# Attention with a token-mixing MLP on one core: a dispatcher orders the engines, and part of the softmax exponentials is computed on VectorE

## The chip, the cores and the metric

The kernel runs on one core of a Trainium2 chip. The core has engines that work side by side, each through its own queue in order: TensorE (PE, matmuls, with weight loads shown as PEld), VectorE (DVE), ScalarE (ACT), GpSimd (POOL) and SyncE (SP, which here only issues DMAs). SBUF is the working memory of 128 partitions; PSUM is the memory that matmuls write, eight banks of 512 f32 columns. The metric is the time of one launch in microseconds (us), the median of several runs. A profile is one execution, whose span runs from the first to the last instruction.

## The reference

With x of 2048 rows by 512 columns, the output is `x + attention(xn) + mixer(xn)`:

```python
xn = _layernorm(x, axis=-1)
# attention: 32 heads of 16
qkv = (xn @ wqkv) ...                       # q, k, v per head
scores = einsum("bhqd,bhkd->bhqk", q, k) * 16 ** -0.5
o = einsum("bhqk,bhkd->bhqd", softmax(scores), v)
A = o.reshape(B, S, D) @ wo
# mixer: over the 2048 rows, with F = 1376
h = _layernorm(xn)
u = gelu(einsum("bsd,sf->bdf", h, w1) + b1) # tanh form
Bx = (einsum("bdf,fs->bds", u, w2) + b2).transpose(0, 2, 1)
```

## The kernel before

The scores are computed transposed: keys on the partitions, queries on the columns. A **block** is one of 4 query ranges of 512 times one of 8 sets of four heads, 32 blocks in all; in a block there are 16 key tiles of 128. One key tile of one block is a **group**, 512 in all. A group has four score matmuls of 32 rows each (`score_group`, L748), one head in each quarter of the array, into two pairs of PSUM banks; two exponentials over 128x1024 on ScalarE (`exp_pair`, L757) into the SBUF ring `pT` of ten buffers; and four matmuls `pv_group` (L767), each writing 32 partitions of PSUM bank 6, over all 16 key tiles. `V17` holds 16 values and a one for each head, so that the 17th row of each result is the softmax's denominator. Six banks form three pairs for scores, bank 6 gathers PV, bank 7 (`EX_BANK`) serves everything else.

At a block's end VectorE copies bank 6 to `OT32` (L688), shuffles the denominator row of each quarter over its 32 partitions (L695) and inverts it in four pieces of 128x128 (L700); GpSimd multiplies (L703) into `oT`. After eight blocks the out-projection (L652) of that query range can run. The mixer runs through bank 7 as well: 11 tasks `ut` (16 matmuls, L605, then a GELU on VectorE and ScalarE), 16 tasks `yt` (11 matmuls, L632, then two VectorE operations into an f32 `resid`), and 16 out-projections. Projections of Q, K and V (L425, L407, L569) are further tasks of that bank. The weights of the mixer are loaded by SP into two slots each (`task_w1_load`, `task_w2_load`); the eight loads of `wo_pad` are in `late_consts`.

The order of each engine's work is written out in Python while the kernel is built. Before, a loop counts periods, one group each: it emits the scores and exponentials of the group, the PV of the group two earlier, and at most two units of other matmuls (`EXTRA_BUDGET`) from a list with start periods (`sched_list`). `Sched` then gives each instruction the semaphore waits that its operands need. It keeps the last writer and the readers of a key, such as `("bank", 7)` or `("wo_pad", 3)`:

```python
        for k in writes:
            w = self.last_writer.get(k)
            if w is not None:
                deps.add(w)
            for r in self.readers.get(k, ()):
                deps.add(r)
```

A DMA is such an instruction too, and what waits for a DMA waits for its landing.

Of the kernel before, what the change touches and what calls it, by code (L numbers as in the profile page):

```python
# [12 lines left out]
S = 2048  # L13
# [13 lines left out]
GELU_A = 0.044715  # L27

DEBUG_SCHED = False
LAG = 2  # L30
NPB = 10
NQS = 3
EXTRA_BUDGET = 2.0
NW1 = 2
NW2 = 2

# [148 lines left out]
def bass_parallel_sum__softmax_full_mha__mixer_token_mlp__prompt_kernel(  # L185
# [18 lines left out]
    with ExitStack() as es:  # L204
# [5 lines left out]
        x_sb = sb("x_sb", [128, NT, D], BF16)  # L210
# [3 lines left out]
        resid = big.bitcast(F32)[:, :].rearrange("p (t d) -> p t d", d=D)  # L214

        def resid_alias_keys(st):
            ks = []
            for j in (2 * st, 2 * st + 1):
                ks.append(("xn", j) if j < NT else ("h", j - NT))
            return ks  # L220
# [6 lines left out]
        V17 = sb("V17", [128, NKT * H * 17 + 16], BF16)  # L227
        pT = sb("pT", [128, NPB, 1024], BF16)
        OT32 = sb("OT32", [128, 2, 512], F32)
        denb = sb("denb", [128, 2, 512], F32)  # L230
# [12 lines left out]
        u_sb = sb("u_sb", [128, 1, 512], F32)  # L243
        ga_sb = sb("ga_sb", [128, 1, 512], F32)
        osb = sb("osb", [128, 2, 512], BF16)
        ps = es.enter_context(nc.psum_tensor("ps", [128, 8 * 512], F32))

# [8 lines left out]
        def bank_bf16(i):  # L256
            return ps.bitcast(BF16)[:, i * 1024:(i + 1) * 1024] if hasattr(ps, "bitcast") else None

# [3 lines left out]
        def dma(q, dst, src, reads, writes, name="", noncontig=False):  # L262
            if noncontig:
                def fn(eng, dst=dst, src=src):
                    with nc.allow_non_contiguous_dma(reason="tiny strided vector load"):
                        return eng.dma_start(dst, src)
            else:
                def fn(eng, dst=dst, src=src):
                    return eng.dma_start(dst, src)
            return sc.add(q, fn, reads=reads, writes=writes, name=name, dma=True)  # L270
# [8 lines left out]
        v17_kh = V17[:, 0:NKT * H * 17].rearrange("p (k h c) -> p k h c", k=NKT, c=17)  # L279
        for T in range(1, 4):  # L280
            sc.add("dve", lambda e, T=T: e.memset(v17_kh[:, :, 8 * T, 0:16], 0.0),
                   writes=[("V", t, T) for t in range(NT)])
        sc.add("dve", lambda e: e.memset(V17[:, NKT * H * 17:], 0.0), writes=[("Vpad",)])
        sc.add("dve", lambda e: e.memset(v17_main[:, :, 16:17], 1.0), writes=[("Vone",)])

        sc.add("pool", lambda e: e.memset(qmask[:, 0:1], 0.0), writes=[("qmask",)])
        for r in range(4):
            sc.add("pool", lambda e, r=r: e.memset(qmask[32 * r:32 * r + 16, 0:1], 1.0),
                   reads=[("qmask",)], writes=[("qmask",)])
        sc.add("pool", lambda e: e.tensor_scalar(qmask[:, 1:2], qmask[:, 0:1], -1.0, 1.0, ALU.mult, ALU.add),  # L290
# [69 lines left out]
        def ln_tile(t, which):  # L360
            ln_stats(t, which)
            ln_norm(t, which)
# [12 lines left out]

        ps_bf = ps.bitcast(BF16)

        def kt_chunk(T, c, bk, evac_eng="dve"):
            kt_pe(T, c, bk)
            kt_evac(T, c, bk, evac_eng)  # L380

        def kt_evac(T, c, bk, evac_eng):
            evac(evac_eng, KT[:, T, 512 * c:512 * (c + 1)], bank(bk), reads=[("bank", bk)],
                 writes=[("KTt", T, t) for t in range(4 * c, 4 * c + 4)])
# [14 lines left out]
        def kt_pe(T, c, bk):  # L399
            for _ in kt_pe_gen(T, c, bk):  # L400
                pass

        def kt_pe_gen(T, c, bk):
            for ct in range(NCT):
                if ct % 2 == 0:
                    yield 2.0
                sc.add("pe", lambda e, ct=ct: e.matmul(  # L407
                    bank(bk), lhsT=wqkv_sb[:, ct, D + 128 * T: D + 128 * T + 128],
                    rhs=xnT[:, ct, 512 * c:512 * (c + 1)], start=(ct == 0), stop=(ct == NCT - 1)),
                    reads=[("wqkv", 1, T)] + [("xnT", t) for t in range(4 * c, 4 * c + 4)], writes=[("bank", bk)])  # L410

        def evac(eng, dst, src, reads, writes):
            if eng == "act":
                return sc.add("act", lambda e: e.activation(dst, src, ACTF.Identity), reads=reads, writes=writes)
            return sc.add("dve", lambda e: e.tensor_copy(dst, src), reads=reads, writes=writes)  # L415

        def qt_proj(qb, T, bk, act_first=False):
            for _ in qt_proj_gen(qb, T, bk, act_first):
                pass

        def qt_proj_gen(qb, T, bk, act_first=False):
            for ct in range(NCT):
                if ct % 2 == 0:
                    yield 2.0
                sc.add("pe", lambda e, ct=ct: e.matmul(  # L425
                    bank(bk), lhsT=wqkv_sb[:, ct, 128 * T:128 * (T + 1)], rhs=xnT[:, ct, 512 * qb:512 * (qb + 1)],
                    start=(ct == 0), stop=(ct == NCT - 1)),
                    reads=[("wqkv", 0, T)] + [("xnT", t) for t in range(4 * qb, 4 * qb + 4)], writes=[("bank", bk)])
            yield 0.0
            for e_ in range(2):  # L430
                b = 8 * qb + 2 * T + e_
                slot = b % NQS
                if act_first and e_ == 0:
                    sc.add("act", lambda e, slot=slot: e.activation(QT[:, slot, :], bank(bk), ACTF.Identity,
                                                                    scale=qmask[:, 0:1]),
                           reads=[("bank", bk), ("qmask",)], writes=[("QT", slot)])
                else:
                    sc.add("dve", lambda e, e_=e_, slot=slot: e.tensor_scalar(QT[:, slot, :], bank(bk),  # L438
                                                                            qmask[:, e_:e_ + 1], None, ALU.mult),
                           reads=[("bank", bk), ("qmask",)], writes=[("QT", slot)])  # L440

        def vT_pe(tiles, T, bk):
            for j, t in enumerate(tiles):
                for ct in range(NCT):
                    sc.add("pe", lambda e, ct=ct, j=j, t=t: e.matmul(  # L445
                        bank(bk)[:, 128 * j:128 * (j + 1)], lhsT=xnT[:, ct, 128 * t:128 * (t + 1)],
                        rhs=wqkv_sb[:, ct, 2 * D + 128 * T:2 * D + 128 * (T + 1)],
                        start=(ct == 0), stop=(ct == NCT - 1)),
                        reads=[("wqkv", 2, T), ("xnT", t)], writes=[("bank", bk)])

        def vT_evac(tiles, T, bk, evac_eng):
            n = len(tiles)
            t0_ = tiles[0]
            assert tiles == list(range(t0_, t0_ + n))
            dst = V17[:, t0_ * H * 17:(t0_ + n) * H * 17].rearrange("p (t h c) -> p t h c", t=n, c=17)[:, :, 8 * T:8 * T + 8, 0:16]
# [3 lines left out]
        NPRE = 4  # L459
        SH = 0  # L460

        def tb(t):
            return t % 2 if t < NPRE else 4

        def vb(t):
            return 2 + (t % 2) if t < NPRE else 5

        def kb(t):
            return PV_BANK if t < NPRE else EX_BANK

        assert NQS >= 2 and (0 % NQS, 1 % NQS) == (0, 1)

        def pro_stage(s_, pre):
            ev = "act" if pre else "dve"

            def ok(t):
                return 0 <= t < NT and (t < NPRE or not pre)

            t = s_ - 5
            if ok(t):  # L480
                if t == NPRE - 1:
                    qt0_evac()
                kt_tile_evac(0, t, kb(t), "dve" if t >= NPRE else ("dve" if t % 2 == 0 else "act"))
                vT_evac([t], 0, vb(t), ev if t % 2 == 0 else "dve")
            t = s_ - 4
            if ok(t):
                kt_tile_pe(0, t, kb(t))
                if t < NPRE:
                    qt0_tile_pe(t)
                vT_pe([t], 0, vb(t))  # L490
            t = s_ - 3
            if ok(t):
                transpose_copy(t, tb(t), ev)
            t = s_ - 2
            if ok(t):
                transpose_pe(t, tb(t))
            t = s_
            if 0 <= t < NT and (t < NPRE + 2 or not pre):
                ln_stats(t, 0)
            t = s_ - 1  # L500
            if 0 <= t < NT and (t < NPRE + 2 or not pre):
                ln_norm(t, 0)
# [14 lines left out]
        NSTG_PRE = NPRE + 5  # L517
        for s_ in range(NSTG_PRE):
            pro_stage(s_, True)

        def block0_work(period):
            s_ = period + NPRE + 2
            if s_ < NSTG_PRE:
                pro_stage_late(s_)
            else:
                pro_stage(s_, False)
# [452 lines left out]
```

## Time and profile before

| | |
|---|---|
| median of 3 runs (lowest, highest) | 982.7 us (981.83, 983.78) |
| span of the profiled execution | 979.6 us |
| ScalarE busy | 953.8 us, 97% |
| TensorE busy | 822.8 us, 84% |
| VectorE busy | 306.4 us, 31% |
| GpSimd busy | 70.1 us, 7% |
| mean granted TensorE clock | 0.807 |
| bytes read from and written to HBM | 15.47 MB, 2.10 MB |

The profile gives one execution only; the median is 3.1 us above its span. A group of instructions is shown as line, engine, operation, output and inputs, shape, and count, then the busy time and the mean length of one, then the engine's idle time just before them and what ended most of it. Matmuls overlap one another, so their mean length is more than the time that each takes of the engine. The clock is what the throttle granted TensorE, 1 being full speed.

### The profile page before, as it was taken

Reading aid. Unit: us, or ns where it says so; the run is one execution under the profiler, and the core shown is the slowest. Engines: PE = TensorE matmul, PEld = TensorE weight load, DVE = VectorE, ACT = ScalarE, POOL = GpSimd, SP = SyncE. Lnnn points to the kernel's source line nnn. Section 1 sums busy time; section 2 is a strip of 40 time slices with the busy share of each in tenths; the row PEclk is TensorE's granted clock in tenths of the full one; section 3 lists DMA queues with packets and bytes.
Section 4 is the critical chain, followed back from the end, with each engine's and each line's share of the span. In section 5 each row is a group of like instructions: output and inputs, shape, how many; then the busy total and the mean of one; then the engine's idle time right before and its main releaser. Section 6 shows DMA issues by size and latency. Waiting matters only on the chain.

```text
span 979.6 us, 11965 instructions
## 1 busy us (share of the span) xinstructions
PE 822.8 (84%) x5019; PEld 208.2 (21%) x5084; DVE 306.4 (31%) x522; ACT 953.8 (97%) x1045; POOL 70.1 (7%) x110
## 2 busy tenths in 40 slices
PE   5888898787888878888888888989889898998885
PEld 3422213211111112222222222111211111111121
DVE  6666633234322343222333223122211212102233
ACT  5999999999999999999999999999999999999995
POOL 3213200000000000000000000000000000000000
PEclk9999859988878888999999999555955555555797
DMA  8000000122111100111011010000000000000000
GB/s 193 2 1 17 6 1 2 22 51 43 21 22 22 22 17 1 30 28 27 11 30 44 17 42 2 0 1 4 19 1 1 1 1 0 1 1 1 11 11 22
DMA packets 57013, 18.34 MB, mean 19 GB/s; under 512 B 50816, under 2 KB 56960, under 8 KB 56960
## 3 DMA queue, kind: packets, MB, share of 16 engines
q1 hardware_dynamic: 53792, 16.00, 7.1%
q10 hardware_dynamic: 3168, 1.57, 0.6%
q8 instruction: 40, 0.66, 0.3%
q14 instruction: 13, 0.11, 0.0%
HBM read 15.47 MB, written 2.10 MB: 18 GB/s over the span
## 4 chain that ended last, share of the span: by engine, by line
ACT 87%; PE 10%; DVE 2%; issue 1%; DMA 1%; ACTq 0%; SPq 0%; DVEq 0%
ACT pT L757 86%; PE ps L748 3%; PE ps L767 2%; PE ps L605 1%; PE ps L425 1%; DMA x_sb<-in_A_x_dram 1%; ACT ga_sb L620 1%; PE ps L389 0%; PE ps L407 0%; DVE denb L717 0%; PE ps L652 0%; DVE QT L438 0%; PE ps L445 0%; DVE osb L665 0%; DVE stats L341 0%
## 5 line engine op out<-in xcount | busy, mean ns | idle before, releaser
L757 ACT ACTIVATE pT<-ps 128x1024 bf16<-128x1024 f32 x1024 | 946.2, 1390 | 4.2 <-PE ps L748 2.6
L748 PE MATMUL ps<-QT,KT 32*128 32x512 bf16 x2048 | 448.9, 464 | 123.5 <-ACT pT L757 102.1
L767 PE MATMUL ps<-pT,V 128*32 128x512 bf16 x2048 | 240.3, 469 | 0.6 <-ACT pT L757 0.6
L748 PEld LDWEIGHTS ps<-QT,KT 32*128 32x128 bf16 x2048 | 95.3, 94 | 505.8 <-ACT pT L757 481.5
L688 DVE COPY OT<-ps 128x512 f32<-128x512 f32 x31 | 21.4, 692 | 322.0 <-PE ps L767 322.0
L700 DVE RECIPROCAL denb<-denb 128x128 f32<-128x128 f32 x124 | 108.8, 920 | 0.9
L703 POOL TENSOR_TENSOR oT<-OT,denb 128x512 bf16<-128x512 f32 x31 | 39.3, 1266 | 791.3 <-DVE denb L700 791.3
L767 PEld LDWEIGHTS ps<-pT,V 128*32 128x32 bf16 x2048 | 51.9, 97 | 148.1 <-issue 145.8
L605 PE MATMUL ps<-big,w1blk 128*128 128x512 bf16 (+1 forms) x158 | 54.5, 419 | 6.5 <-issue 3.6
L632 PE MATMUL ps<-gT,w2blk 128*128 128x512 bf16 (+1 forms) x160 | 53.0, 398 | 2.8 <-issue 1.8
L637 DVE SCALAR_TENSOR_TENSOR big<-ps,x_sb 128x512 f32<-128x512 f32 x16 | 11.1, 691 | 102.3 <-PE ps L632 102.3
L652 PE MATMUL ps<-wo_pad,oT 128*128 128x512 bf16 x107 | 35.5, 406 | 2.4 <-issue 1.7
L610 DVE TENSOR_SCALAR u_sb<-ps,b1col 128x512 f32<-128x512 f32 (+1 forms) x11 | 8.3, 751 | 74.3 <-PE ps L605 74.3
L438 DVE TENSOR_SCALAR QT<-ps,qmask 128x512 bf16<-128x512 f32 x30 | 21.1, 747 | 32.3 <-PE ps L425 32.3
L665 DVE TENSOR_TENSOR osb<-ps,big 128x512 bf16<-128x512 f32 x16 | 11.0, 688 | 52.1 <-PE ps L652 52.0
L425 PE MATMUL ps<-xnT,wqkv_sb 128*128 128x512 bf16 x49 | 21.4, 509 | 2.6 <-issue 2.6
L695 DVE STREAM_SHUFFLE denb<-OT 128x512 f32<-128x512 f32 x31 | 22.4, 721 | 0.0
L415 DVE CAST V<-ps 128x128 bf16<-128x128 f32 (+1 forms) x26 | 12.4, 477 | 22.8 <-PE ps L569 22.2
L347 POOL TENSOR_TENSOR mv<-mv,mhalf 128x1 f32<-128x1 f32 x32 | 18.2, 567 | 2.7
L407 PE MATMUL ps<-xnT,wqkv_sb 128*128 128x512 bf16 x42 | 14.7, 423 | 2.7 <-DVE KT L415 1.6
L605 PEld LDWEIGHTS ps<-big,w1blk 128*128 128x128 bf16 (+1 forms) x176 | 10.7, 101 | 28.4 <-issue 24.4
L415 DVE CAST KT<-ps 128x128 bf16<-128x128 f32 (+1 forms) x26 | 12.2, 469 | 14.4 <-PE ps L407 9.1
(59 smaller groups left out, 211.8 us busy)
## 6 DMA issues: line engine op xcount, KB each, us to landing
w1blk<-in_B_w_dram SPq DMA_DIRECT2D x10, 512.0 KB, 4.1
w2blk<-in_B_w_dram SPq DMA_DIRECT2D x16, 320.0 KB, 3.3
out_dram<-osb SPq DMA_DIRECT2D x16, 128.0 KB, 1.7
x_sb<-in_A_x_dram SPq DMA_DIRECT2D x3, 512.0 KB, 9.9
wqkv_sb<-in_A_wqkv_dram ACTq DMA_DIRECT2D x3, 384.0 KB, 11.2
wo_pad<-in_A_wo_dram SPq DMA_DIRECT2D x8, 64.0 KB, 2.0
wqkv_sb<-in_A_wqkv_dram ACTq DMA_DIRECT2D x3, 128.0 KB, 3.8
w2blk<-in_B_w_dram SPq DMA_DIRECT2D x16, 24.0 KB, 1.7
```

What stands on the lines that cost most here:

```text
L415: return sc.add("dve", lambda e: e.tensor_copy(dst, src), reads=reads, writes=writes)
L425: sc.add("pe", lambda e, ct=ct: e.matmul(bank(bk), lhsT=wqkv_sb[:, ct, 128 * T:128 * (T + 1)], rhs=xnT[:, ct, 512 * qb:512 * (qb + 1)], st ...
L605: sc.add("pe", lambda e, st=st: e.matmul(bank(EX_BANK)[0:m, :], lhsT=w1blk[:, slot, st, 0:m], rhs=h_sb[:, st, :], start=(st == 0), stop=(s ...
L632: sc.add("pe", lambda e, ft=ft, m=m: e.matmul(bank(EX_BANK), lhsT=w2blk[0:m, slot, ft, :], rhs=gT[0:m, ft, :], start=(ft == 0), stop=(ft = ...
L652: sc.add("pe", lambda e, G=G: e.matmul(bank(EX_BANK), lhsT=oT[:, par, G, 128 * sti:128 * (sti + 1)], rhs=wo_pad[:, G, :], start=(G == 0), ...
L688: sc.add("dve", lambda e: e.tensor_copy(OT32[:, eb, :], bank(PV_BANK)), reads=[("bank", PV_BANK)], writes=[("OT32", eb)])
L695: sc.add("dve", lambda e: e.stream_shuffle(denb[:, eb, :], OT32[:, eb, :], [16] * 32), reads=[("OT32", eb)], writes=[("denb", eb, c) for c ...
L700: sc.add("dve", lambda e, cs=cs: e.reciprocal(denb[:, eb, cs], denb[:, eb, cs]), reads=[("denb", eb, c)], writes=[("denb", eb, c)])
L703: sc.add("pool", lambda e: e.tensor_tensor(oT[:, qb % 2, G, :], OT32[:, eb, :], denb[:, eb, :], ALU.mult), reads=[("OT32", eb)] + [("denb" ...
L748: sc.add("pe", lambda e, r=r, bk=bk: e.matmul(bank(bk), lhsT=KT[32 * r:32 * r + 32, T, 128 * kt:128 * (kt + 1)], rhs=QT[32 * r:32 * r + 32 ...
L757: sc.add("act", lambda e: e.activation(pT[:, buf, :], ps[:, s_ * 1024:(s_ + 1) * 1024], ACTF.Exp, scale=0.25), reads=[("bank", 2 * s_), (" ...
L767: sc.add("pe", lambda e, r=r, buf=buf, off=off: e.matmul(bank(PV_BANK)[32 * r:32 * r + 32, :], lhsT=V17[:, off:off + 32], rhs=pT[:, buf, 5 ...
```

## The change

The loop over periods is replaced by a dispatcher, `Dispatch`, which runs while the kernel is built. It keeps a time for each engine, adds an assumed duration (`EST`) for each instruction, and whenever an engine is free in its own reckoning gives it the ready step of the smallest priority number. What it decides is the order of the instructions of each engine; the waits come from `Sched` as before. Tasks of bank 7 have due times, counted in groups scored; while none is due, the bank goes to a new kind of work.

That work, a **unit**, is one group whose exponentials are computed on VectorE; it is taken from key tiles 2, 6, 10 and 14 of blocks from 2 on, and 59 of the 512 groups become units. Their four score matmuls go one by one through bank 7, either beside a pair of ordinary scores in another quarter of the array or alone after 0.3 us in the reckoning. VectorE turns each into the 16 bits of a bf16 number with one addition (the scores are scaled beforehand by `QSCALE`, in `qmask`), then corrects the mantissa with four operations over 2048 columns. The correction is a sum of three terms, and TensorE adds them: a unit has three rounds of PV matmuls, two with `V17` and one with a scaled copy, `VS`.

The denominators are no longer shuffled. Four DMAs take each quarter's row of 512 from one partition to 32 partitions by 16 columns, one reciprocal of 128x16 inverts them, a DMA writes them to a DRAM scratch, and four DMAs read them back, each row to 32 partitions.

Other changes: both halves of Q are evicted by one operation of 1024 columns; `ut` is scaled so that the mixer's second product and the out-projection accumulate in one bank (`task_out`, one VectorE operation for each of 16 row tiles in place of three or so); x is loaded again for that sum, since its place is used by the units. The prologue and the last block's end are as before, with one more memset (`VS`, on GpSimd).

```diff
-LAG = 2
-NQS = 3
-EXTRA_BUDGET = 2.0
+NQS = 4
+D_KTS = (2, 6, 10, 14)
+D_FROM = 2
+D_SOLO = 0.3
+D_AHEAD = 5
...
+EST = dict(
+    start=15.5, pe_switch=0.11, mm512=0.215, mm128=0.065, pe_lat=0.25,
+    exp=0.924, exp_lat=1.45, tanh=0.75, act_lat=0.55,
+    dve_lat=0.05, p1=0.70, ts4=0.62, tt2=1.15, cp512=0.70, cp1024=1.2, cp128=0.30,
+    stats=0.92, norm=0.45, xcopy=0.43, small=0.25, stt=0.70,
+    pool_lat=0.1, rstd=0.95, pmul=1.3, sp=0.15, dma=2.3, dma_big=6.0,
+)
...
+            def gather():
+                for r in range(4):
+                    dma("sp", rl[32 * r:32 * r + 32, eb, :],
+                        OT32[32 * r + 16:32 * r + 17, eb, :].rearrange("p (j c) -> p j c", c=16),
+                        reads=[("OT32", eb)], writes=[("rl", eb)], name="den_gather", noncontig=True)
+                at[("rl", b)] = dp.use("sp", 4 * EST["sp"]) + EST["dma"]
+            yield ("sp", 0.5, lambda: done(("ot", b)), gather)
+
+            def recip():
+                sc.add("dve", lambda e: e.reciprocal(rl[:, eb, :], rl[:, eb, :]),
+                       reads=[("rl", eb)], writes=[("rl", eb)])
+                at[("rc", b)] = dp.use("dve", EST["small"]) + EST["dve_lat"]
+            yield ("dve", 0.6, lambda: done(("rl", b)), recip)
...
+                dma("sp", scr[eb].rearrange("r (j c) -> (r j) c", c=16), rl[:, eb, :],
+                    reads=[("rl", eb)], writes=[("scr", eb)], name="den_put", noncontig=True)
...
+                for r in range(4):
+                    dma("sp", denb[32 * r:32 * r + 32, :], scr[eb, r:r + 1, :].broadcast_to([32, 512]),
+                        reads=[("scr", eb)], writes=[("denb",)], name="den_spread")
...
+                sc.add("dve", lambda e: e.tensor_scalar(bv_i[:, i, 512 * r:512 * (r + 1)], bank(EX_BANK),
+                                                        EXP_BIAS, 0.0, ALU.add, ALU.max),
+                       reads=[("bank", EX_BANK)], writes=[("bD", i)] + extra)
...
+                sc.add("dve", lambda e: e.tensor_scalar(ge_i[:, 0, :], bv_i[:, i, :], 0x7F, 0x3F80,
+                                                        ALU.bitwise_and, ALU.bitwise_or),
...
+                sc.add("dve", lambda e: e.tensor_tensor(ge_f[:, 1 + i, :], bv_f[:, i, :], ge_f[:, 0, :], ALU.mult),
...
+                sc.add("dve", lambda e: e.tensor_tensor(ge_f[:, 1 + i, :], ge_f[:, 1 + i, :], ge_f[:, 0, :], ALU.mult),
...
+                sc.add("dve", lambda e: e.tensor_scalar(bv_i[:, 2 + i, :], bv_i[:, i, :], 0x7F80, None,
+                                                        ALU.bitwise_and),
...
+                            u = pend["unit"]
+                            if u is not None:
+                                rs = [r for r in u["left"] if r // 2 != hf]
+                                if rs:
+                                    d_score(u, rs[0])
...
+                            pv_round(b, lambda r: V17[:, voff(r, kt):voff(r, kt) + 32],
+                                     lambda r: bv_f[:, i, 512 * r:512 * (r + 1)],
...
+                            pv_round(b, lambda r: V17[:, voff(r, kt):voff(r, kt) + 32],
+                                     lambda r: bv_f[:, 2 + i, 512 * r:512 * (r + 1)],
...
+                            pv_round(b, lambda r: VS[:, voff(r, j):voff(r, j) + 32],
+                                     lambda r: ge_f[:, 1 + i, 512 * r:512 * (r + 1)],
...
+            nb = 8 * qb + 8 if qb < NQB - 1 else 8 * qb + 6
+            dl = NKT * (nb + 2) + 22.0 * sti if qb < NQB - 1 else NKT * (nb + 0.5) + 4.0 * sti
```

## The prediction

> **What bounds the kernel now.** I read the page's first part, the costliest groups, the chain, then the vector engine's and the sync engine's own rows, then the tensor engine by stretches.
>
> ```profile
> PE 822.8 (84%) x5019; PEld 208.2 (21%) x5084; DVE 306.4 (31%) x522; ACT 953.8 (97%) x1045; POOL 70.1 (7%) x110
> ...
> PEclk9999859988878888999999999555955555555797
> ...
> ACT pT L757 86%; PE ps L748 3%; PE ps L767 2%; PE ps L605 1%; PE ps L425 1%; DMA x_sb<-in_A_x_dram 1%; ACT ga_sb L620 1%; PE ps L389 0%; PE ps L407 0%; DVE denb L717 0%; PE ps L652 0%; DVE QT L438 0%; PE ps L445 0%; DVE osb L665 0%; DVE stats L341 0%
> ...
> L757 ACT ACTIVATE pT<-ps 128x1024 bf16<-128x1024 f32 x1024 | 946.2, 1390 | 4.2 <-PE ps L748 2.6
> ...
> L700 DVE RECIPROCAL denb<-denb 128x128 f32<-128x128 f32 x124 | 108.8, 920 | 0.9
> ```
>
> ScalarE is the bound: 97% busy, 86% of the chain, and its exponentials lost 4.2 us in idle time. One of them holds the engine for 946.2/1024 = 0.924 us (the 1390 is the length of one, which overlaps the next). VectorE is idle for two thirds of the span. The clock row matters later: late in the span the granted clock is half.
>
> **What the change takes away.** 59 of the 512 groups leave ScalarE, two exponentials each: 118 x 0.924 = 109.0 us. The first exponential starts at 15.79 us in the timeline of before and runs without a gap from 22.5 us on; the added memset on GpSimd (nearest row: 128x2048 in 1.80 us) falls into 1.65 us in which GpSimd waits for VectorE, so the start may move by 0.3 us at most, and I take 0. The tail from the last exponential to the end is the same sequence. So if ScalarE stays as dense, the span is 979.6 - 109.0 = 870.6 us. The median, 982.7, lies 3.1 us above the profiled span; I add the same 3.1 to get a time: 873.7. All else is what ScalarE loses.
>
> **VectorE's work.** Removed: 108.8 us of reciprocals and 22.4 of shuffles, 7.8 (L640) and about 12 us of merged evictions of QT and of the results. Added: 31 reciprocals of 128x16 (between 0.18, the row of the smallest statistics operation, and 0.92, L700 with eight times the columns; I take 0.25, 8 us) and 59 units. A unit has four evictions of 512 PSUM columns, 0.69 each by L688 (2.8 us), and four operations over 2048 bf16 columns, which the trace does not show. Their ends: 0.69, as if 512 f32 columns (L613) took as long as 2048, and 4 x 0.69 = 2.77 each. The nearest row is line 356 (bf16, SBUF to SBUF): 512 columns in 0.39. Another 1536, at two or four columns in the 1.35 ns that L613 needs for one (0.69/512), add 1.0 or 0.5: 1.4 or 0.9. I take 1.2 for each: 4.8. A unit is 7.6 us, 59 are 448; between 5.5 and 13.9 us a unit at the ends. VectorE is then busy 306 - 151 + 8 + 448 = 611 us of some 930: not the bound as a sum.
> [...]
>
> **VectorE's order, and a wait it did not have.** The new epilogue brings four denominator rows from one partition each to 32 partitions with four DMAs, inverts, writes to DRAM, and spreads with four more. All four gathers write the key ("rl", eb), all four spreads ("denb",). Sched.add makes a writer depend on the last writer of its key, and a DMA is no exception, so each of the four waits until the one before has landed. Before has exactly this pattern in the eight loads of wo_pad:
>
> ```profile
> SPq L269 <- DMA wo_pad<-in_A_wo_dram: 11.9, 7, 1.7
> ```
>
> ```profile
> 85.63 14.55 SPq L269 DMA_DIRECT2D wo_pad<-in_A_wo_dram  x8
> ```
>
> The first is a wait of the sync queue (total, times, longest), the second its timeline: eight in 14.55 us, 1.82 us each, seven of them waiting 1.7 us for the one before. Four gathers thus take 7.3 us from the copy of the PV bank to the last landing. The dispatcher, which writes every engine's order, allows 4 x 0.15 + 2.3 = 2.9 us, and puts the reciprocal into VectorE's queue there. VectorE works in order, so it stands for 7.3 - 2.9 = 4.4 us at nearly every block's end, 30 times. That is 132 us, and with 611 busy still below the span; but what is queued behind is the next eviction of the extra bank (bits of a unit, or K, V, Q, MLP), and behind that, in TensorE's strict order, the next score matmul into that bank, and behind that the score pairs for ScalarE.
> How much reaches ScalarE: three pairs of banks, one being read, so two scored pairs ahead, 2 x 0.924 = 1.85 us of cover. While a unit holds the extra bank, its rounds need VectorE every 1.6 us (0.3 until the dispatcher stops waiting for a ride, 0.33 for a matmul step as in the timeline of before around 701 us, 0.28 until its reader starts, as before the first exponentials, 0.69 for the eviction), so TensorE stops soon after VectorE does: 4.4 - 1.85 = 2.5 us lost. 59 units x 4 x 1.6 = 378 us of some 830 us after the first blocks: about half of the boundaries. At the others the bank is filled by some ten chunks of other matmuls that need no VectorE for up to 10 us: I take 0.4. Mean 1.45, times 30 = 43 us. Ends: 0 (the cover holds), and 2.2 us a transfer (the 0.2 KB row of b1c) exposed at every boundary: 30 x (8.8 - 2.9 - 1.85) = 122 us.
> Sync's own queue: gather, put and spread are nine serial transfers, 16 us of a block's 27 (870/32). Weight loads behind them land up to 10 us later than planned; their cover is the time between two uses of a slot, 6 groups (11 us) for w1 and 22 (40 us) for w2, and I take 0; without it each late load would cost its lateness less 1.85. At the end there is one place without such cover: the fourth query block's out-projection is due half a block after block 29, whose o^T needs copy 0.7 + 7.3 + 0.3 + 1.8 + 7.3 + product 1.3 = 19 us; half a block is 14. 5 us lost.
>
> **TensorE.** A unit adds three PV rounds where one was; the score rounds are the same 4 x 32-row matmuls, which run beside a pair when they ride.
>
> ```profile
> 833.00:882.00 49.00, 44.68 (x215) 0.50 0.00 1
> 917.00:966.00 49.00, 41.27 (x267) 0.99 0.03 11
> ```
>
> ```profile
> 850.38 1.35 PE L748 MATMUL ps<-QT,KT 32*128 32x512 bf16 x4
> 851.66 0.62 PE L767 MATMUL ps<-pT,V 128*32 128x512 bf16 x4
> ...
> 855.32 1.04 PE L767 MATMUL ps<-pT,V 128*32 128x512 bf16 x8
> ```
>
> The first fence is the stretches view (length, PE busy and matmuls, granted clock): with scores and PV alone the clock is 0.50, with out-projections between them 0.99. The second is the timeline at 0.50: a second PV round adds 1.04 - 0.62 = 0.42 us. Two score steps of 0.53 and one PV of 0.55 fill 1.61 of a group's 1.84 us: 0.23 us to spare. A unit at half clock asks for 3 x 0.42 = 1.26, and with half its scores alone 2 x 0.42 more, 2.1 us; the groups per unit, 453/59 = 7.7, spare 1.77. The shortfall, 0.33 us, counts for the some 40 units away from the dense matmuls: 13 us. Ends: 0 (full clock) and 40 x 2.1 = 84.
> [...]
>
> **Sum.** 979.6 - 109.0 + 43 + 13 + 5 = 931.6, plus 3.1 around the span: **934.7 us**, taken as 935.
>
> **Rivals.**
> A. The wait at the reciprocal is covered. For it: VectorE has a third of the time free, and ScalarE's present idle time is 4.2 us. Against it: two pairs are 1.85 us and the wait is 4.4. Then 873.7 + 13 = 887.
> B (slower). The gathers' wait is exposed at every block's end. Each boundary may cost 109.0/30 = 3.6 us before the gain is gone; the point is a gather of 2.9 + 1.85 + 3.6 = 8.4 us, 2.1 us a transfer. For it: 2.2 us for the smallest load; against: 1.7 us for results and small weights (w2blk, 24 KB), and boundaries without a unit. At 2.2: 873.7 + 122 = 996.
> C. The wide vector operations run at their upper end: VectorE is busy 983 us and waits 132: about 1,115. Against it: the 0.39 of L356.
> D. The order comes out such that ScalarE's removed work is replaced by other waits almost evenly, 981 to 985.
>
> **Chances.** Forecast (900 to 980) 0.54, A 0.23, B 0.15, C 0.05, D 0.03. Range 880 to 1000: it leaves out the third of A below 880 (0.07), C (0.05) and a third of B (0.05). Faster by over 0.2% (what a measurement of this kernel can tell): 0.54 + 0.23 = 0.77; within: 0.03; slower: 0.20.
>
> **What would show it.** Exponentials x906 at 0.92 us of engine time. Right: VectorE's wait for rl from DMA, about 30 times, mean near 4.4 us; idle time before the exponentials near 60 us, named PE or, behind it, VectorE's evictions; sync waiting on rl and denb transfers 3 + 3 times a block. Wrong: no such wait (A), wide operations above 2 us (C), a clock near 1 in the late slices (TensorE's term 0), or more than 100 us of idle ScalarE (B).

## The result, and the profile after

The kernel before takes 982.3 us (median of 4 runs, 981.3 to 983.8), the changed kernel 1091.6 us (4 runs, 1085.1 to 1128.0): a ratio of 1.111 with a 95% interval of 1.104 to 1.118. Some executions of a kernel are slower at a lower granted clock (here 1085.1 us at 0.677 and 1128.0 at 0.638), so all medians, ratios and differences of times from here on are over those within 1.5% of the kernel's fastest. The forecast was 935, its range 880 to 1000: the sign was wrong. The changed kernel's profiled execution is the longest of the four, 1128.0 us with a span of 1126.2; what is read from its rows goes with that span.

The page of the changed kernel, the lines that answer to those shown of before: busy times, granted clock, the chain by line, then groups.

```profile
PE 973.4 (86%) x5498; PEld 230.8 (20%) x5556; DVE 543.1 (48%) x796; ACT 875.2 (78%) x927; POOL 75.5 (7%) x111
...
PEclk8566568559665566556666656656566757656798
...
PE ps L583 22%; PE ps L666 15%; DMA rl<-OT 14%; ACT pT L637 12%; PE ps L1072 6%; PE ps L1004 5%; DVE xreg L821 4%; PE ps L1077 2%; DVE big L845 2%; PE ps L487 1%; DMA wo_pad<-in_A_wo_dram 1%; DVE big L851 1%; DVE OT L751 1%; PE ps L926 1%; PE ps L944 1%
...
L637 ACT ACTIVATE pT<-ps 128x1024 bf16<-128x1024 f32 x906 | 865.4, 1068 | 228.1 <-PE ps L583 225.1
...
L845 DVE TENSOR_TENSOR big<-xreg,big 128x2048 bf16<-128x2048 bf16 x59 | 72.9, 1235 | 1.7
...
L767 DVE RECIPROCAL rl<-rl 128x16 f32<-128x16 f32 x31 | 7.8, 253 | 133.5 <-DMA rl<-OT 133.5
...
L857 DVE TENSOR_SCALAR xreg<-xreg 128x2048 int16<-128x2048 int16 x59 | 44.4, 753 | 0.0
L838 DVE TENSOR_SCALAR big<-xreg 128x2048 int16<-128x2048 int16 x59 | 42.2, 715 | 1.9
```

The 118 exponentials are gone (906 are left), and ScalarE is no longer the bound: its exponentials wait 228.1 us, where they waited 4.2 before, nearly all of it for score matmuls. These two rows carry the whole difference of the spans: 979.6, less 80.8 of exponentials (946.2 to 865.4), plus 223.9 of idle time, is 1122.7 of 1126.2.

Two things in the page can hold scores back. VectorE stands 133.5 us at the reciprocal, 31 times, for the gathers, which are 14% of the chain. And TensorE is granted five or six tenths of its clock in most slices, from the second on, where before it had eight or more in most of the first two thirds; its busy time grew by 150.6 us and its matmuls are 37% of the chain in two lines.

How TensorE comes to stay at half clock shows at the start. The stretches view, 4 us each, before and then after; columns are stretch, length, busy time and instructions of TensorE, its weight loads, VectorE, ScalarE and GpSimd, then the granted clock, DMA share and GB/s.

```profile
20.00:24.00 4.00, 4.00 (x38) 2.52 (x36) 2.66 (x9) 3.02 (x4) 1.47 (x4) 0.57 1.24 238
24.00:28.00 4.00, 3.78 (x45) 2.01 (x42) 3.93 (x13) 3.96 (x5) 1.64 (x5) 1.00 0.08 14
```

```profile
20.00:24.00 4.00, 4.00 (x28) 1.80 (x28) 2.62 (x8) 2.88 (x3) 1.24 (x3) 0.50 1.19 230
24.00:28.00 4.00, 4.00 (x32) 1.82 (x28) 3.34 (x10) 3.24 (x5) 0.86 (x3) 0.50 0.03 7
```

Before is at half clock for most of the first of these stretches (0.57 in the mean) and at 1.00 in the second. The changed kernel is at 0.50 in both and stays there until past 56 us, busy without a gap, and ScalarE starves (3.24 us busy in the second stretch, 3.96 before). There are no units yet in block 0, and no gather has been issued (the first comes at 62.97 us). So something else in the order of TensorE's work must differ. The timeline of TensorE, in a stretch where both kernels run dense `ut` matmuls beside the scores; first before, then after. Columns: start, length of the run of like instructions, engine, line, operation, and how many.

```profile
229.50 0.61 PE L748 MATMUL ps<-QT,KT 32*128 32x512 bf16 x4
230.04 1.03 PE L605 MATMUL ps<-big,w1blk 128*128 128x512 bf16 x2
231.01 0.82 PE L748 MATMUL ps<-QT,KT 32*128 32x512 bf16 x4
```

```profile
232.14 0.61 PE L583 MATMUL ps<-QT,KT 32*128 32x512 bf16 x2
232.68 1.03 PE L1004 MATMUL ps<-big,w1blk 128*128 128x512 bf16 x2
233.65 0.61 PE L583 MATMUL ps<-QT,KT 32*128 32x512 bf16 x2
```

Before, the four score matmuls of a group stand next to each other in the queue. When TensorE is late and both bank pairs are already free, all four quarters of the array run in one pass: four in the 0.54 us from 229.50 to 230.04. After, the dispatcher puts dense matmuls between the two pairs of a group, since at full clock each pair only becomes runnable one exponential after the other (at 1.00, the second pair at 234.89 us in before waits 0.26 us for ScalarE); late, at half clock, a pair takes the same 0.54 us as the four. One pair and two dense matmuls repeat every 1.51 us (232.14 to 233.65). A pair feeds one exponential, which needs 0.924. So there are two suspects, the serial gathers and this order, beside the units themselves.

### The profile page after: what moved, and what is told of

Read it like the earlier page. It is cut to its first block, busy times and chain, and to the rows that moved or that the text cites. A ratio compares the mean times of both kernels' runs of the same rounds, so it can differ in the third digit from the quotient of the medians.

```text
span 1126.2 us, 13430 instructions
## 1 busy us (share of the span) xinstructions
PE 973.4 (86%) x5498; PEld 230.8 (20%) x5556; DVE 543.1 (48%) x796; ACT 875.2 (78%) x927; POOL 75.5 (7%) x111
## 4 chain that ended last, share of the span: by engine, by line
PE 55%; DMA 16%; DVE 14%; ACT 12%; issue 2%; POOL 1%; SPq 0%; ACTq 0%; DVEq 0%
PE ps L583 22%; PE ps L666 15%; DMA rl<-OT 14%; ACT pT L637 12%; PE ps L1072 6%; PE ps L1004 5%; DVE xreg L821 4%; PE ps L1077 2%; DVE big L845 2%; PE ps L487 1%; DMA wo_pad<-in_A_wo_dram 1%; DVE big L851 1%; DVE OT L751 1%; PE ps L926 1%; PE ps L944 1%
## 5 line engine op out<-in xcount | busy, mean ns | idle before, releaser
L637 ACT ACTIVATE pT<-ps 128x1024 bf16<-128x1024 f32 x906 | 865.4, 1068 | 228.1 <-PE ps L583 225.1
L583 PE MATMUL ps<-QT,KT 32*128 32x512 bf16 x2048 | 485.1, 530 | 105.0 <-DVE xreg L821 72.6
L821 DVE TENSOR_SCALAR xreg<-ps 128x512 int16<-128x512 f32 x236 | 161.6, 685 | 121.2 <-PE ps L583 119.5
L845 DVE TENSOR_TENSOR big<-xreg,big 128x2048 bf16<-128x2048 bf16 x59 | 72.9, 1235 | 1.7
L851 DVE TENSOR_TENSOR big<-big 128x2048 bf16<-128x2048 bf16 x59 | 72.1, 1223 | 0.7
L767 DVE RECIPROCAL rl<-rl 128x16 f32<-128x16 f32 x31 | 7.8, 253 | 133.5 <-DMA rl<-OT 133.5
L666 PE MATMUL ps<-xreg,V 128*32 128x512 bf16 x472 | 59.7, 600 | 0.1
L857 DVE TENSOR_SCALAR xreg<-xreg 128x2048 int16<-128x2048 int16 x59 | 44.4, 753 | 0.0
L838 DVE TENSOR_SCALAR big<-xreg 128x2048 int16<-128x2048 int16 x59 | 42.2, 715 | 1.9
L666 PE MATMUL ps<-big,VS 128*32 128x512 bf16 x236 | 36.0, 601 | 0.0
L487 PE MATMUL ps<-wqkv_sb,xnT 128*128 128x128 bf16 x256 | 29.1, 265 | 3.9 <-DVE QT L934 3.9
```

The source lines that it names most:

```text
L583: sc.add("pe", lambda e: e.matmul(bank(bk), lhsT=KT[32 * r:32 * r + 32, T, 128 * kt:128 * (kt + 1)], rhs=QT[32 * r:32 * r + 32, sl, :], st ...
L637: sc.add("act", lambda e: e.activation(pT[:, buf, :], ps[:, s_ * 1024:(s_ + 1) * 1024], ACTF.Exp, scale=EXP_SCALE), reads=[("bank", 2 * s_ ...
L666: sc.add("pe", lambda e, r=r, lhs=lhs, rhs=rhs: e.matmul(bank(PV_BANK)[32 * r:32 * r + 32, :], lhsT=lhs, rhs=rhs, start=first, stop=last, ...
L821: sc.add("dve", lambda e: e.tensor_scalar(bv_i[:, i, 512 * r:512 * (r + 1)], bank(EX_BANK), EXP_BIAS, 0.0, ALU.add, ALU.max), reads=[("ban ...
L838: sc.add("dve", lambda e: e.tensor_scalar(ge_i[:, 0, :], bv_i[:, i, :], 0x7F, 0x3F80, ALU.bitwise_and, ALU.bitwise_or), reads=[("bD", i)], ...
L845: sc.add("dve", lambda e: e.tensor_tensor(ge_f[:, 1 + i, :], bv_f[:, i, :], ge_f[:, 0, :], ALU.mult), reads=[("bD", i), ("gD",)], writes=[ ...
```

## The experiments

Each kernel ran four times (e5 five times), and the range behind a median spans all these runs; the kernel before took 983.5 to 984.2 us on the same chips. Ratios are to it. The expectations number their theories. Theory 1 is the prediction's: the serial gathers stop VectorE, and that stops TensorE and ScalarE. Theory 2: TensorE at half clock is the bound, because the units load it too much. Theory 3: the dispatcher's order of the score matmuls leaves TensorE short at half clock.

**e1: the gathers and spreads in parallel.** Each of the four DMAs gets a key of its own, and the readers name all four.

```diff
-                        reads=[("OT32", eb)], writes=[("rl", eb)], name="den_gather", noncontig=True)
+                        reads=[("OT32", eb)], writes=[("rl", eb, r)], name="den_gather", noncontig=True)
...
-                        reads=[("scr", eb)], writes=[("denb",)], name="den_spread")
+                        reads=[("scr", eb)], writes=[("denb", r)], name="den_spread")
```

> The changed kernel with one edit: each of the four gathers and each of the four spreads has a key of its own, so they no longer wait for one another; the order of every engine is unchanged. Theory 1 (VectorE stands at the reciprocal for serial gathers and drags TensorE and ScalarE with it): VectorE's wait for rl falls from 133 us to below 40, and the time falls by most of the surplus, to 900 to 960 us, with the clock up. Theory 2 (TensorE at half clock is the bound, and the waits only lie beside it): the wait falls as much, but the time stays above 1040 us and the clock below 0.72.

Measured: 1006.7 us (997.6 to 1018.3), ratio 1.020 (1.015 to 1.026), between the two expected ranges. The waits of the changed kernel, then those of e1; total, times, longest, in us.

```profile
ACT pT L637 <- PE ps L583: 225.1, 263, 14.0
...
DVE rl L767 <- DMA rl<-OT: 133.5, 31, 13.1
```

```profile
ACT pT L637 <- PE ps L583: 126.3, 181, 10.5
...
DVE rl L767 <- DMA rl<-OT: 39.1, 18, 10.0
```

In e1 VectorE still waits for the gathers 18 times, but for 39.1 us in all. The median fell by 85 us; between the two profiled executions VectorE's wait fell by 94 us and ScalarE's by 99. The serial transfers are a cause, and a large one; but 126.3 us of idle ScalarE remain and the clock is still 0.69. It is not the only one.

**e2: the dispatcher is told how long the serial transfers take**, so that nothing waits that could have been put ahead.

```diff
-                at[("rl", b)] = dp.use("sp", 4 * EST["sp"]) + EST["dma"]
+                at[("rl", b)] = dp.use("sp", 3 * 1.85) + 1.85
...
-                at[("denb", b)] = dp.use("sp", 4 * EST["sp"]) + EST["dma"]
+                at[("denb", b)] = dp.use("sp", 3 * 2.0) + 2.0
```

> The changed kernel with the dispatcher told the serial durations (7.4 us for the gathers, 8.0 us for the spreads): the transfers stay serial, only the place of the reciprocal in VectorE's queue and what depends on it move. Theory 1: VectorE's wait for rl falls below 60 us, the time as in the run with parallel transfers within 30 us. Theory 2: above 1040 us, clock below 0.72.

Measured: 970.8 us (966 to 1017), ratio 0.987 (0.981 to 0.992), 61 units. In this kernel the dispatcher ended ahead of the last row tile's out-projection task, which is left out (17 matmuls of some 5,500). The wait at the reciprocal is 32.7 us and ScalarE still waits 110.7 us for scores. So the transfers may stay serial: what makes VectorE wait is its place in an in-order queue, taken too early. How much of the time that alone is worth isn't shown, since the dispatcher, told other durations, also ordered the rest anew.

**e3 and e4: no units**, the changed kernel and e1 with `D_FROM` past the last block.

```diff
-D_FROM = 2
+D_FROM = 99
```

> The changed kernel without units: all 512 groups are exponentiated on ScalarE, the denominators still go through serial DMAs. Its floor is that of the kernel before, 982 us. Theory 1: the reciprocal's wait stays (about 130 us), but with no unit in the extra bank only a part reaches ScalarE: 1000 to 1040 us. Theory 2: without units TensorE has less to do and the clock is as before, 0.8: 982 to 1000 us. If the dispatcher's order itself is the cause (a third theory), the clock stays below 0.72 and the time above 1040 us even without units.

> No units and parallel transfers: what is left is the dispatcher's order. Theories 1 and 2: 980 to 995 us, clock about 0.8. Third theory (the order itself): above 1030 us, clock below 0.72.

Measured: e3 1099.4 us (1096 to 1123), ratio 1.117 (1.113 to 1.121); e4 1037.6 us (1035 to 1104; it scatters too much for an interval). With all 1024 exponentials back on ScalarE, the dispatcher's order and the serial transfers are still 12% slower than before, and with parallel transfers the order is slower by 53 us. Theory 2 falls: the units are not what slows the kernel. In the changed kernel they gave back 8 us (1099.4 to 1091.6) of the 109 that they take from ScalarE; with parallel gathers 31 (1037.6 to 1006.7).

**e5, e6, e7: a group's scores kept together.** The dispatcher may put nothing between the first and second score pair of a group: `unlocked()` becomes a condition of PV rounds, of a unit's lone scores, of the dense chunks and of the prologue's tile steps. The dispatcher also goes on as long as a task of bank 7 is left. e5 is the changed kernel with this, e6 is e1 with this, e7 is e6 without units.

```diff
+        lock = {"on": False}
+        def unlocked():
+            return not lock["on"] or len(pbuf) < 2
...
+                            lock["on"] = hf == 0
...
-                    return pv_state["b"] < NBLK and is_free("pv") and bool(pv_cands())
+                    return unlocked() and pv_state["b"] < NBLK and is_free("pv") and bool(pv_cands())
...
-                    yield ("pe", 1.2, lambda: True, go)
+                    yield ("pe", 1.2, unlocked, go)
```

> The changed kernel, but the dispatcher may put nothing between the two score pairs of a group (TensorE's queue gets four scores in a row, as before); transfers stay serial; the dispatcher then finds room for 49 units instead of 59, so the floor rises by 10 x 1.85 to 892 us. Theory 3 (the second pair's matmuls can no longer run beside the first's when TensorE is late, so that it never catches up at half clock): the clock rises above 0.75 and the time falls to 930 to 1000 us, the rest being the reciprocal's wait. Theory 1 (the wait alone is the cause): no less than 1060 us.

> Parallel transfers and four scores in a row, 49 units, floor 892 us. Theories 1 and 3 together: 900 to 945 us, clock above 0.75, faster than both kernels. If TensorE's load by units is a cause of its own: above 960 us with a clock below 0.7.

> No units, parallel transfers, four scores in a row: only the dispatcher's other choices remain against the kernel before. Theory 3: 980 to 1000 us, clock near 0.8. If the order hurts in another way: as without this edit, above 1030 us.

Measured: e5 991.0 us (987.6 to 992.0), ratio 1.007 (1.005 to 1.010); e6 944.0 us (943.2 to 944.4), ratio 0.960 (0.958 to 0.962); e7 993.7 us (990.7 to 997.7), ratio 1.011 (1.008 to 1.015), its clock 0.73 where 0.8 was expected. The dispatcher makes 49 units in e5 and e6 (the locked order leaves less room), so their exponentials cost 20 x 0.924 = 18.5 us more than in the changed kernel, and the time still falls by 101 us and 63 us. The scatter falls to 0.1% in e6.

The page of e6, busy times, clock and exponentials:

```profile
PE 825.9 (88%) x5476; PEld 216.0 (23%) x5476; DVE 478.5 (51%) x716; ACT 867.6 (92%) x947; POOL 74.2 (8%) x111
...
PEclk8988579798778787896876765767875677958798
...
L644 ACT ACTIVATE pT<-ps 128x1024 bf16<-128x1024 f32 x926 | 858.5, 1148 | 49.2 <-PE ps L589 48.3
```

And its TensorE timeline at the place shown above:

```profile
235.17 0.61 PE L589 MATMUL ps<-QT,KT 32*128 32x512 bf16 x4
235.71 1.89 PE L1012 MATMUL ps<-big,w1blk 128*128 128x512 bf16 x4
237.53 0.61 PE L589 MATMUL ps<-QT,KT 32*128 32x512 bf16 x4
```

Four scores again in 0.54 us, and TensorE's busy time is back at 826 us from 973, with nearly the same number of matmuls: the 147 us more in the changed kernel were the same work at a lower clock and in half-filled passes (in e5, with serial transfers, TensorE is busy 166.4 of the 200 us from 190 on, in the changed kernel 181.7). In e5 VectorE still waits 143.2 us for the gathers, more than in the changed kernel, and yet it takes 991. Counted from e6, the serial transfers alone cost 47 us, the order alone 63, and both together 148.

The start tells the order from the transfers as well. The second slice of the clock row is 9 in e6 (23.5 to 47.1 us) and 5 in the changed kernel (28.2 to 56.3 us). The units begin with block 2 and the changed kernel issues its first gather only at 62.97 us, so neither holds its clock down there.

**e8: the kernel before, with only this order changed.** The hand-written loop emits the first pair of a group, its exponential, the PV, then the second pair and its exponential. No unit, no new DMA, no dispatcher.

```diff
-                score_group(period)
+                score_group(period, (0, 1))
...
-                exp_pair(2 * period + 1)
...
+            if NKT <= period < NGRP:
+                score_group(period, (2, 3))
+                exp_pair(2 * period + 1)
```

> The kernel before with one edit: the second score pair of a group, with its exponential, is put behind the PV of an earlier group, so that two pairs no longer stand in a row. Theory 3: TensorE no longer catches up at half clock: the clock falls below 0.72, the time rises above 1010 us. Theories 1 and 2: 980 to 990 us, since nothing is added.

Measured: 1116.6 us (1111 to 1146), ratio 1.135 (1.131 to 1.139), clock 0.61. Its page; then, from the stretches view of TensorE alone (stretch, length, busy time and matmuls, granted clock, DMA share, GB/s), 200 us of its middle, and the same stretch of before; last its timeline.

```profile
PE 1035.2 (93%) x5084; PEld 221.2 (20%) x5084; DVE 306.8 (28%) x522; ACT 989.6 (89%) x1045; POOL 70.3 (6%) x110
...
PEclk8999555565556565555555599955555555555567
...
L757 ACT ACTIVATE pT<-ps 128x1024 bf16<-128x1024 f32 x1024 | 980.0, 1225 | 97.9 <-PE ps L748 86.5
```

```profile
190.00:390.00 200.00, 195.00 (x838) 0.54 0.12 25
```

```profile
190.00:390.00 200.00, 163.07 (x993) 0.85 0.12 25
```

```profile
231.47 0.61 PE L748 MATMUL ps<-QT,KT 32*128 32x512 bf16 x2
232.01 0.62 PE L767 MATMUL ps<-pT,V 128*32 128x512 bf16 x4
232.56 0.61 PE L748 MATMUL ps<-QT,KT 32*128 32x512 bf16 x2
233.10 1.03 PE L605 MATMUL ps<-big,w1blk 128*128 128x512 bf16 x2
234.07 0.61 PE L748 MATMUL ps<-QT,KT 32*128 32x512 bf16 x2
```

This one edit of the order, with as many matmuls as before (5,084 weight loads in both), costs 133 us, more than the whole change. TensorE is busy 195 of 200 us and gets fewer matmuls done (838 for 993), and its clock comes back only for short spells.

**e9 and e10: idle matmuls to hold the clock.** Two dense matmuls whose result is overwritten stand ahead of a group's scores where the period before had no other dense work: in before (e9) and in e8 (e10). They test theory 4: that the granted clock follows the share of the array in use. My estimates were a clock above 0.93 and 980 to 988 us for e9, above 0.85 and 985 to 1020 us for e10.

```diff
+            if warm[0] and rs[0] == 0:
+                wb = 2 * pslot(2 * g)
+                for _ in range(2):
+                    sc.add("pe", lambda e, wb=wb: e.matmul(bank(wb), lhsT=wqkv_sb[:, 0, 0:128], rhs=xnT[:, 0, 0:512],
+                                                           start=True, stop=True),
```

> The kernel before, with two idle matmuls of 128x128 by 512 columns (written to a score bank that the next score overwrites) ahead of a group's scores wherever the previous period held no extra matmuls. [...]

> The same idle matmuls in the kernel before whose score pairs were set apart (that run: 1117 us, clock 0.61). [...] If pairs set apart are slow by themselves, or a low clock cannot be left: 1110 us or more.

Measured: e9 977.2 us (975.8 to 977.5), ratio 0.994 (0.992 to 0.995); e10 1056.5 us (1049 to 1082), ratio 1.073 (1.068 to 1.078), its clock 0.84. The clock rows of e9 and e10:

```profile
PEclk9999999999999999999999999999999999999999
```

```profile
PEclk9999999555599999755557559689999999999998
```

More work makes before a little faster and holds its clock at 0.987. In e10 the split order is fine as long as the clock is up; when it falls, it sticks at half (four slices of 26.4 us on end). That is where the estimate missed: the idle matmuls keep the clock from falling in quiet stretches (1.00 from 833 to 882 us in e9, 0.50 in before), but don't bring it back in e10, where the order doesn't fill the array.

**e11 and e12: towards a better version.** e11 is e6 with one idle matmul ahead of a group where no dense work ran in the last 1.5 us. e12 is e11 with a key of its own for each of the eight `wo_pad` loads and with the gather's allowance at 4.2 us.

```diff
-                at[("rl", b)] = dp.use("sp", 4 * EST["sp"]) + EST["dma"]
+                at[("rl", b)] = dp.use("sp", 4 * 0.5) + 2.2
...
-                    dma("sp", dst, src, reads=[], writes=[("wo_pad", g) for g in range(NG)], name="ld_wo")
+                    dma("sp", dst, src, reads=[("wo_z",)], writes=[("wo_pad", g, 4 * e_ + r) for g in range(NG)], name="ld_wo")
```

> The fastest kernel so far (parallel transfers, four scores in a row, 49 units: 944 us, clock 0.78) with one idle matmul ahead of a group's scores where no dense matmul ran in the dispatcher's last 1.5 us. [...] If the waits at the extra bank are what is left: 935 to 950 us whatever the clock.

> As the run with one idle matmul, and the eight loads of wo_pad have keys of their own (they no longer hold the sync queue for 15 us ahead of a gather), and the dispatcher allows 4.2 instead of 2.9 us for a gather. VectorE's wait for rl falls from 49 us to below 20; the time by 5 to 20 us against the run without this: 890 to 925 us. If the rest of the wait lies beside other work: no difference beyond 5 us.

Measured: e11 953.5 us (947.8 to 956.7), ratio 0.970 (0.965 to 0.975): the clock rose from 0.78 to 0.88, and the kernel is no faster than e6, but 9 us slower; my estimate was 905 to 932. e12 938.5 us (934.3 to 943.4), ratio 0.955 (0.950 to 0.959): 15 us less than e11, the size expected of the two edits, though not within 890 to 925. Its median is the lowest here, 4.5% ahead of before, but its interval overlaps e6's. The reason for the `wo_pad` edit is in the sync queue of the changed kernel, in its timeline:

```profile
98.53 15.10 SPq L361 DMA_DIRECT2D wo_pad<-in_A_wo_dram  x8
113.67 5.77 SPq L360 DMA_DIRECT2D rl<-OT  x4
```

The second block's gathers stood behind eight loads that wait for one another: VectorE stood 13.1 us at the reciprocal, TensorE behind it 12.9 us, from before 110 to past 122 us, and ScalarE 14.0. The waits of e12 that answer to those shown above (29.9 us for the gathers, where below 20 was expected):

```profile
DVE rl L781 <- DMA rl<-OT: 29.9, 12, 4.5
...
ACT pT L651 <- PE ps L589: 39.5, 47, 3.2
```

## Why the prediction was wrong

Medians of the four combinations, in us:

| | pairs apart (dispatcher's order) | four scores in a row |
|---|---|---|
| serial transfers | 1091.6 (the change, 59 units) | 991.0 (e5, 49 units) |
| transfers in parallel | 1006.7 (e1, 59 units) | 944.0 (e6, 49 units) |

**The step that failed is TensorE's**: "The shortfall, 0.33 us, counts for the some 40 units away from the dense matmuls: 13 us". I priced what a unit adds, and only away from dense work, because I took the full clock for granted beside it. I did not price the order in which the dispatcher puts the scores that were there before, although the diff shows the pairs fed one by one (`hf`) with other steps between. Two score steps apart fit a group at half clock (my 1.61 of 1.84 us) only while nothing dense is among them; with two dense matmuls a group takes 2.60 us (e8). Before escapes this since its two steps shrink to one when TensorE is late. Measured, the order costs 63 us with parallel transfers (e1 to e6) and 101 with serial ones (the change to e5), in spite of ten units less each time. That before, with that order alone, becomes slower than the changed kernel (e8) shows the mechanism by itself. No rival held it. B's sign, over 100 us of idle ScalarE, was there (228.1), but not its cause: a transfer of 2.1 us or more. Four gathers take 5.77 us to the last issue and 1.7 to land, 7.5 where I had 7.3.

**The clock** I read as given by the kind of work: 0.50 with scores and PV alone, 0.99 beside dense matmuls. The changed kernel is granted 0.50 beside dense matmuls too (the start, above), and e8, with them, 0.54 over 200 us of which TensorE is busy 195: being busy isn't enough either.

**The wait at the reciprocal** was right in kind and size: 132 us in 30 waits predicted, 133.5 in 31 measured (4.3 us each). Its price to ScalarE, 43 us, was too small: it is 85 us in the order that the change has (the change to e1). Where a group's scores stand together it is 47 (e5 to e6); that this lies near 43 isn't shown to be more than luck, for the shares taken for boundaries with and without a unit were not measured. In the change's order a stop of VectorE ends in a stop of TensorE (the score matmuls wait 72.6 us for VectorE's evictions of the extra bank, 37 times), and what comes after is often run at half clock (0.50 from 122 to 160 us, behind the stop that ends at 122; 0.60 in the mean from 190 to 390). That link between the two causes is read from the traces and fits the table; no run isolates it.

**The removed exponentials**, −109.0, came to −80.8 of engine time. One is 0.955 us in the mean instead of 0.924: spread over the 263 waits that the trace counts, the missing 28.2 are 0.107 us for each exponential that starts after a gap (a lone one takes 1.02 in the timeline). In e6, with fewer gaps, one is 0.927. The term was right only while ScalarE stays dense.

**The wide vector operations**, taken as 1.2 each, are 0.715, 0.753, 1.235 and 1.223: 3.9 us for the four. The two or four columns in 1.35 ns behind the 1.2 were an estimate; over 2048 columns, 0.715 us is 0.35 ns a column and 1.235 us 0.60. With four evictions of 0.685 a unit is 6.7 us, and VectorE is busy 543 us where I had 611. The reciprocal is 0.253 (0.25 taken). None of it changed the outcome; C is excluded.

**The other terms.** Weight loads behind the gathers were costed at 0, and the waits list none of TensorE for one; but the other way round it cost time, since the second block's gathers stood behind the loads of `wo_pad`. The 5 us at the end was not measured separately. Where both causes are mended (e6), the time is 52 us above 982.3 − 98 x 0.924 = 891.7; 45 of it are idle time before the exponentials (49.2 us, 4.2 before). That remainder was not in my sum, except for the 5 and what the 13 stood for. e11 shows that it isn't simply the clock: its exponentials wait as long for scores as e6's (47.8 us, 48.3 in e6), and of the 8 us by which its span is longer some 7 are the GELU on ScalarE, which waits 9.0 us for VectorE instead of 2.3; VectorE itself waits 63.3 us for the gathers, 49.0 in e6. e12's two edits take 15 us off e11, which leaves it 5.5 below e6. Why VectorE is later in e11, and what the last 47 us are (39.5 of ScalarE's idle time in e12 is waiting for scores), stays open.

## What to carry to other kernels

An order that is packed for the fast state of an engine has to be looked at in its slow state too: matmuls that use a part of the array belong next to each other in the queue, so that they can share a pass when they are late (four scores in the 0.54 us of two; 63 us from e1 to e6), even if at full speed they become ready one by one. When a planner writes the order, check its assumed durations against the trace first for what stands ahead in an in-order queue; give each of several DMAs into one buffer a key of its own, or place the consumer where the last of them has landed. And when an edit moves work to another engine, make one run with the reordering and without the moved work: e3 and e4 would have shown at once that the new work was not the cost, and that the order alone had one.

## What the runs showed of the hardware

In the stretches measured here the granted clock goes with how much of the array is in use, not with how long TensorE is busy. From 833 to 882 us before runs scores and PV alone: busy 44.68 of 49 us with 215 matmuls, granted 0.50. e9, with two idle matmuls ahead of each group's scores there, is busy 42.37 us with 265, granted 1.00. From 190 to 390 us e8 is busy 195.00 of 200 us with 838 matmuls at 0.54, before 163.07 us with 993 at 0.85. From 228 to 240 us the changed kernel's TensorE has no gap (40 matmuls) and is granted 0.50.

How much of the array an order uses can be estimated from the timelines. One more dense matmul takes 0.43 us at half clock (two take 0.97 us, four 1.82, in the timelines above) and counts as all of the array for that time; four scores or four PV matmuls count as 0.43 too, and a pair of scores, on two quarters of the array, as half of that, 0.215.

- The changed kernel's pair and two dense matmuls use (0.215 + 0.86)/1.51 = 0.71 of the array; it is granted 0.50 from 228 to 240 us, where it runs them.
- e8's pair, PV, pair and two dense matmuls use (0.215 + 0.43 + 0.215 + 0.86)/2.60 = 0.66; it is granted 0.54 in the mean from 190 to 390 us.
- PV, two dense matmuls and four scores in a row take 2.06 us in before (225.92 to 227.98), which is (0.43 + 0.86 + 0.43)/2.06 = 0.83; its clock goes from 0.50 there to 1.00 from 232 us on. e6, with four scores in a row too, goes the same way: they take 0.54 us at 235.17 and 0.32 at 239.47.

At full clock one more dense matmul takes half as long, 0.215 us (two take 0.54 in before at 235.54, four 0.97 in e6 at 239.79). Scores and PV alone are then (0.215 + 0.215)/1.85 = 0.23 of a group's time. Where before comes to that, from 239.75 to 245.65 us, the clock goes from 1.00 (240 to 242 us) to 0.54 (242 to 244). With e9's two idle matmuls, 0.215 each, it is 0.47, and e9 is granted 0.987 over its whole span. The shares are my estimates; at which share the clock changes, and how long that takes, isn't settled by these runs.
